# Chunked linear attention with two MLPs: loads in order of use into separate memory, and low words of the weight conversion in PSUM banks

## The chip, the core and the metric

The kernel runs on one core of one Trainium2 chip. The metric is the device time of one execution in microseconds (us), the median of several runs. The engines are TensorE (PE in the profile; PEld is its weight load), VectorE (DVE), ScalarE (ACT), GpSimd (POOL) and SyncE (SP), which only issues DMAs here. Each works through its own queue of instructions in order and waits for other engines by semaphores.

## The reference, cut to what matters

```python
# attention: B=2, H=8, S=768, D=64; blocks of 64 with a decaying state
intra = einsum(qb, kb) * Dmask          # lam ** (i - j), lower triangle
out   = intra @ vb + (qb * lam_pow) @ kv_state
kv_state = lam ** 64 * kv_state + (kb * rev_pow).T @ vb
x = out as [1536 tokens, 512]
# first MLP
h = x @ w_in                            # 512 -> 2048
x = (h * clip(h + 3, 0, 6) / 6) @ w_out # 2048 -> 512
# second MLP
h = x @ w2_in
P = a0 + a1 h + a2 h^2 + a3 h^3;  Q = 1 + |b0| |h| + |b1| h^2
y = (P / (Q + 1e-6)) @ w2_out
```

The four weight matrices are 64-bit floats in device memory, all other inputs 32-bit floats.

## The kernel before

**Attention.** The kernel uses chunks of 128 positions, 12 of them (6 for each batch entry), all 8 heads at once. For chunk c:
- `load_nat` issues the DMAs of q, k, v into tiles `qn`, `kn`, `vn` of which there are two each, so that a load waits until the chunk two before is done with its tile.
- `att_t`: TensorE transposes q and k into two banks (L339, L344), ScalarE copies them to `qT`, `kT`. GpSimd makes `qd` = q scaled (L349) and `kd` = k scaled (L352). Chunks 0 and 6 have no `qd`, chunks 5 and 11 no `kd`.
- `att_s`: the scores (L362) into two banks, which VectorE masks into `at` (L366, two halves).
- `att_o`: into bank X the product of the state with `qd` (L381) and of `at` with v (L389); into bank Y the product of `kd` with v (L386). In the text o(c).
- `att_state`: VectorE adds Y to the state (L398, L400); GpSimd makes the decayed state `sd` (L403).
- `att_x`: ScalarE copies X to `xh` (L413), VectorE subtracts to get the remainder `xl` (L414). Each large product is done in three passes, high by high, low by high, high by low.

t(c), s(c), at(c), qd(c) and so on in the text are these pieces for chunk c.

**Weights.** They come as jobs, `load_job(j)`: one or two blocks of 512 KB as raw 64-bit words, into tiles `raw0` and `raw1` of which there are two each. Jobs 0 and 1 have one block, the others one of w_in and one of w_out. A block is turned into two 32-bit parts in pieces:
- `conv_c`: ScalarE scales the high words (L153), VectorE clamps them (L154, "the clamp").
- `conv_s`: ScalarE reduces the low words in place in the raw tile (L176), VectorE shifts and joins (L177, two SBUF operands). `conv_l` is the same with the low words in bank X or Y (L163, L164); before, the main loop alone uses it.
- `conv_w`: VectorE puts the sign in (L194), which after `conv_s` comes from the raw tile.
- `conv_h`: ScalarE copies to the high part `wih` or `woh` ("hi", L207), GpSimd subtracts to get the low part `wil` or `wol` (L208).

**MLP steps.** `mm1(s)` multiplies input block s into bank `hb[s % 2]` (L216, L218, L220), `act1` applies the activation (L268 ScalarE, L271 VectorE), `act_fin` splits it into `gh` (L280) and `gl` (L281, GpSimd), `mm2` adds to the four `acc` banks (L235).

**Order.** Everything is under a manual schedule: each engine's queue is in program order. First attention chunks 0 to 4 (scores alternate between `acc[0:2]` and `acc[2:4]`, transposes use `hb`), then eight steps s = 0 to 7 that mix chunk 4 + s, mm1(s + 1), mm2(s - 1) and the conversion of job s + 3; here scores and transposes use X and Y. From s = 1 on TensorE runs mm1(s + 1), t(c), half of mm2(s - 1), s(c), the other half, o(c). Then comes the main loop of MLP steps alone. PSUM has eight banks: `acc` (4), `hb` (2), X, Y.

Of the kernel before, what the change touches and what calls it, by code (L numbers as in the profile page):

```python
# [19 lines left out]
LAG2 = 3  # L20
WARM = (6, 2, 3)
SIGN = 0x80000000
# [8 lines left out]
def fused_kernel(  # L31
# [51 lines left out]

    EIN, EOUT = 11, 9
    w_tiles(wp, range(EIN), range(EOUT))

# [38 lines left out]
    def load_job(j):  # L125
        if j >= len(jobs):
            return
        t = []
        for m, f in jobs[j]:
            r = rp.tile([128, KD, 128, 2], U32, name=f"raw{m % 2}")  # L130
            if m % 2 == 0:
                nc.sync.dma_start(
                    r.rearrange("p k f t -> p k (f t)"),
                    w32[m].rearrange("(k p) f -> p k f", p=128)[:, :, 256 * f : 256 * f + 256],
                )
            else:
# [172 lines left out]
    with ExitStack() as actx:  # L309
        ap = actx.enter_context(tc.tile_pool(name="ap", bufs=1))  # L310
        lamb = ap.tile([128, H], F32, name="lamb")
# [12 lines left out]
        def load_nat(c, which):  # L324
            b, s0 = c // CPB, (c % CPB) * CH
            for nm in which:
                x = ap.tile([128, H, D], F32, name=nm + "n", bufs=2)
                src = {"q": q, "k": k, "v": v}[nm]
                nc.sync.dma_start(x, src[b, :, s0 : s0 + CH, :].rearrange("h s d -> s h d"))
                nat.setdefault(c, {})[nm] = x  # L330

        def att_t(c, bk, between=None):
            qn, kn, vn = (nat[c][nm] for nm in "qkv")
            qT = ap.tile([128, NP, CH], F32, name="qT")
# [35 lines left out]

        Xv = X.rearrange("p (a b) -> p a b", a=NP)
        Yd = Y[:, 0 : 64 * NP].rearrange("p (a b) -> p a b", a=NP)
        decayed = {}

        def att_o(c):
            at, qd, kd, vn = live[c]
            cs = [slice(128 * p, 128 * p + 128) for p in range(NP)]

            if qd is not None:
                for p in range(NP):  # L380
                    nc.tensor.matmul(X[:, cs[p]], lhsT=state[:, p, :], rhs=qd[:, p, :], start=p == 0, stop=False,  # L381
                                     skip_group_check=True)
            halves = [(p, h2, slice(64 * h2, 64 * h2 + 64)) for p in range(NP) for h2 in range(2)]
            if kd is not None:
                for p, h2, r in halves:
                    nc.tensor.matmul(Yd[r, p, :], lhsT=kd[:, 2 * p + h2, :], rhs=vn[:, 2 * p + h2, :],  # L386
                                     start=True, stop=True)
            for p, h2, r in halves:
                nc.tensor.matmul(X[r, cs[p]], lhsT=vn[:, 2 * p + h2, :], rhs=at[:, h2, p, :],  # L389
                                 start=qd is None and p == 0, stop=p == NP - 1, skip_group_check=True)  # L390

        def att_state(c):
            if c % CPB == CPB - 1:
                return
            for h2 in range(2):
                r = slice(64 * h2, 64 * h2 + 64)
# [11 lines left out]
        def att_x(c):  # L408
            del live[c]
            o = CH * (c % CPT)  # L410
            hi = xh[c // CPT][:, :, o : o + CH]
# [4 lines left out]
        with tc.manual_schedule():  # L416
            load_nat(0, "qk")
            nc.scalar.dma_start(lamb, lam.unsqueeze(0).to_broadcast([128, H]))
            load_nat(1, "qk")
            load_nat(0, "v")  # L420
            nc.vector.memset(warm, 0.0)
            nc.vector.memset(c3, 3.0)
# [10 lines left out]

            warm_up(WARM[0])
            for h2 in range(2):
                r = slice(64 * h2, 64 * h2 + 64)
                nc.vector.tensor_copy(lamq[r, :], lamb.rearrange("p (a b) -> p a b", b=2)[r, :, h2])
            for p in range(NP):
                nc.vector.tensor_tensor_scan(
                    out=qtab[:, p, :], data0=lamq[:, p : p + 1].to_broadcast([128, CH]), data1=zero,  # L440
                    initial=1.0, op0=ALU.mult, op1=ALU.add)
                for h2 in range(2):
                    hd = 2 * p + h2
                    nc.vector.tensor_tensor_scan(
                        out=dmat[:, h2, p, :], data0=lamb[:, hd : hd + 1].to_broadcast([128, CH]), data1=ident,
                        initial=0.0, op0=ALU.mult, op1=ALU.add)
            for h2 in range(2):
                nc.vector.tensor_copy(ktab[:, :, h2], dmat[:, h2, :, CH - 1])

# [3 lines left out]


            att_t(0, hb, lambda: warm_up(WARM[1]))
            warm_up(WARM[2])
            load_nat(2, "qk")
            load_nat(1, "v")
            att_s(0, acc[0:2])
            load_job(0)  # L460
            att_t(1, hb)
            att_o(0)
            att_state(0)
            att_x(0)
            load_nat(2, "v")
            load_nat(3, "qk")
            load_job(1)
            att_s(1, acc[2:4])
            att_t(2, hb)
            conv_all(conv_c, 0)  # L470
            conv_all(conv_s, 0)
            conv_all(conv_w, 0)
            att_o(1)
            att_state(1)
            att_x(1)
            conv_all(conv_h, 0)
            load_nat(3, "v")
            load_nat(4, "qk")
            load_job(2)
            att_s(2, acc[0:2])  # L480
            att_t(3, hb)
            conv_all(conv_c, 1)
            conv_all(conv_s, 1)
            conv_all(conv_w, 1)
            att_o(2)
            att_state(2)
            att_x(2)
            conv_all(conv_h, 1)
            load_nat(4, "v")
            load_job(3)  # L490
            load_nat(5, "qk")
            nc.sync.dma_start(a_sb, a_dram.unsqueeze(0).to_broadcast([128, 4]))
            nc.sync.dma_start(b_sb, b_dram.unsqueeze(0).to_broadcast([128, 2]))
            att_s(3, acc[2:4])
            att_t(4, hb)
            load_nat(6, "qk")
            att_o(3)
            att_state(3)
            att_x(3)
            conv_all(conv_c, 2)  # L500
            conv_all(conv_s, 2)
            load_nat(5, "v")
            att_s(4, acc[0:2])
            conv_all(conv_w, 2)
            conv_h(2, 0)
            conv_h(2, 1)

            att_steps = NCH - CPT
            for s in range(att_steps):
                c = CPT + s  # L510
                j = s + 3
                load_job(j + 1)
                if s == 0:
                    mm1(0)
                    act1(0)
                    att_o(c)
                    att_state(c)
                    att_x(c)
                    act_fin(0)
                    conv_all(conv_c, j)  # L520
                    conv_all(conv_s, j)
                    mm1(1)
                    act1(1)
                else:
                    mm1(s + 1)
# [8 lines left out]
                    if s == 1:  # L534
                        conv_all(conv_w, j - 1)
                    conv_all(conv_h, j - 1)
# [4 lines left out]
                    conv_all(conv_s, j)  # L541
                    mm2(s - 1, (2, 3))
                    att_o(c)
                    att_state(c)
                    att_x(c)
# [5 lines left out]
    wq = ctx.enter_context(tc.tile_pool(name="wq", bufs=1))  # L551
    w_tiles(wq, range(EIN, NF), range(EOUT, NF))
# [92 lines left out]
```

## Time and profile before

| | |
|---|---|
| median of 3 runs | 602.67 us (602.53 to 602.83) |
| profiled execution | 602.82 us, span of its instructions 600.9 us |
| busy, share of the span | PE 588.1 us (98%), PEld 480.6 (80%), DVE 445.2 (74%), ACT 384.0 (64%), POOL 366.8 (61%) |
| granted TensorE clock | 1.00 in all slices |
| DMA | 46.68 MB, mean 78 GB/s; 39104 of 61289 packets under 512 B |

Matmuls are pipelined, so one matmul's row lasts longer than the distance to the next; the start times tell the pace. In rows of a timeline the columns are start, duration, engine, line, operation, output and inputs, count, and in brackets the idle time before with what ended it. "<-" in a row of waits separates who waited from what it waited for.

### The profile page before, as it was taken

What the parts mean: (1) busy time and instruction counts of PE and PEld (TensorE: products, weight loads), DVE (VectorE), ACT (ScalarE), POOL (GpSimd) and SP (SyncE); (2) the same over time, 40 slices, a digit from 0 to 9 for tenths busy, and PEclk for the clock granted to TensorE, in tenths of its full rate; (3) what the DMA queues carried; (4) which work ended last, traced back from release to release, by engine and by line L of the source; (5) the groups of instructions that cost most, each with busy time, mean ns of one, the idle gap of its engine ahead of it and who ended that gap; (6) DMA issues with size and microseconds to landing.
All of it is one profiled execution on the core that took longest, in us unless ns stands there. A gap on an engine that the chain in (4) does not pass through costs nothing.

```text
span 600.9 us, 8288 instructions
## 1 busy us (share of the span) xinstructions
PE 588.1 (98%) x3035; PEld 480.6 (80%) x3035; DVE 445.2 (74%) x476; ACT 384.0 (64%) x635; POOL 366.8 (61%) x291
## 2 busy tenths in 40 slices
PE   8898999999999999999999999999999999999997
PEld 5786888888888888888888787877788888888886
DVE  5877888787411011488888899999999888999991
ACT  2566465677422222588787877787887767877771
POOL 3756677566421222266676677688776677777772
PEclk9999999999999999999999999999999999999999
DMA  8987755364000000266655000000010000100001
GB/s 169 267 214 196 173 157 160 130 211 150 1 1 0 1 0 1 88 206 197 184 171 172 1 1 35 1 0 2 28 43 0 2 0 2 69 2 0 1 1 71
DMA packets 61289, 46.68 MB, mean 78 GB/s; under 512 B 39104, under 2 KB 55744, under 8 KB 61248
## 3 DMA queue, kind: packets, MB, share of 16 engines
q1 hardware_dynamic: 60960, 46.02, 26.9%
q8 instruction: 24, 0.39, 0.3%
q10 hardware_dynamic: 288, 0.14, 0.1%
q14 instruction: 17, 0.14, 0.1%
HBM read 43.00 MB, written 3.15 MB: 77 GB/s over the span
## 4 chain that ended last, share of the span: by engine, by line
PE 52%; DVE 24%; ACT 4%; issue 3%; POOL 1%; DVEq 0%; ACTq 0%
PE acc L235 26%; DVE Y L304 8%; PE hb L216 8%; PE hb L220 8%; PE hb L218 8%; DVE ta L154 2%; DVE X L164 2%; DVE ta L194 2%; DVE Y L164 2%; DVE tb L294 2%; DVE tb L194 2%; ACT ta L153 1%; DVE td L305 1%; DVE tb L154 1%; DVE raw L184 1%
## 5 line engine op out<-in xcount | busy, mean ns | idle before, releaser
L304 DVE RECIPROCAL Y<-tb 128x512 f32<-128x512 f32 x48 | 161.3, 3360 | 1.6
L281 POOL TENSOR_TENSOR gl<-td,gh 128x512 fp32r<-128x512 f32 x84 | 111.2, 1324 | 77.1 <-ACT gh L280 76.0
L216 PE MATMUL hb<-xh,wih 128*128 128x512 f32 x384 | 104.3, 393 | 0.5 <-ACT td L293 0.4
L218 PE MATMUL hb<-xh,wil 128*128 128x512 f32 x384 | 102.7, 389 | 0.0
L220 PE MATMUL hb<-xl,wih 128*128 128x512 f32 x384 | 102.6, 389 | 0.0
L295 POOL TENSOR_TENSOR tc<-ta,tc 128x512 f32<-128x512 f32 x48 | 62.2, 1295 | 58.2 <-ACT tc L292 58.2
L271 DVE SCALAR_TENSOR_TENSOR td<-tc,hb 128x512 f32<-128x512 f32 x48 | 32.8, 683 | 84.3 <-ACT tc L268 84.3
L216 PEld LDWEIGHTS hb<-xh,wih 128*128 128x128 f32 x384 | 71.1, 188 | 17.4 <-ACT td L293 1.8
L218 PEld LDWEIGHTS hb<-xh,wil 128*128 128x128 f32 x384 | 72.1, 188 | 15.2
L220 PEld LDWEIGHTS hb<-xl,wih 128*128 128x128 f32 x384 | 72.1, 188 | 15.0
L268 ACT ACTIVATE tc<-hb,c 128x512 f32<-128x512 f32 x48 | 32.9, 686 | 71.7 <-PE hb L220 71.6
L235 PE MATMUL acc<-gh,woh 128*128 128x512 f32 x192 | 76.1, 396 | 0.0
L235 PE MATMUL acc<-gl,woh 128*128 128x512 f32 x192 | 74.8, 390 | 0.0
L235 PE MATMUL acc<-gh,wol 128*128 128x512 f32 x192 | 74.8, 389 | 0.0
L280 ACT CAST gh<-td 128x512 fp32r<-128x512 f32 x84 | 52.0, 619 | 25.9 <-DVE td L271 13.8
L296 POOL TENSOR_TENSOR td<-td,tc 128x512 f32<-128x512 f32 x48 | 63.8, 1330 | 3.8
L208 POOL TENSOR_TENSOR wil<-ta,wih 128x512 fp32r<-128x512 f32 x32 | 41.4, 1294 | 34.7 <-ACT wih L207 34.7
L289 ACT ACTIVATE X<-hb,b_sb 128x512 f32<-128x512 f32 x48 | 31.8, 662 | 42.8 <-PE hb L220 34.1
L235 PE MATMUL acc<-woh,gl 128*128 128x512 f32 x144 | 56.5, 392 | 1.1 <-POOL gl L281 1.1
L235 PE MATMUL acc<-woh,gh 128*128 128x512 f32 x144 | 56.2, 390 | 0.3 <-ACT raw L253 0.3
L235 PE MATMUL acc<-wol,gh 128*128 128x512 f32 x144 | 56.0, 389 | 0.0
L208 POOL TENSOR_TENSOR wol<-tb,woh 128x512 fp32r<-128x512 f32 x29 | 38.4, 1324 | 14.4 <-ACT woh L207 14.4
(104 smaller groups left out, 1029.1 us busy)
## 6 DMA issues: line engine op xcount, KB each, us to landing
raw<-in_moe_w_in_dram SPq DMA_DIRECT2D x32, 512.0 KB, 3.8
raw<-in_moe_w_out_dram SPq DMA_DIRECT2D x32, 512.0 KB, 4.6
qn<-in_q_dram SPq DMA_DIRECT2D x12, 256.0 KB, 5.5
kn<-in_k_dram SPq DMA_DIRECT2D x12, 256.0 KB, 5.3
vn<-in_v_dram SPq DMA_DIRECT2D x12, 256.0 KB, 4.8
out_dram<-raw SPq DMA_DIRECT2D x11, 256.0 KB, 2.2
out_dram<-raw ACTq DMA_DIRECT2D x1, 128.0 KB, 1.8
out_dram<-raw SPq DMA_DIRECT2D x1, 128.0 KB, 1.7
```

The source lines that it names most:

```text
L208: nc.gpsimd.tensor_tensor(lo, x, hi.bitcast(F32), op=ALU.subtract)
L216: nc.tensor.matmul(h, lhsT=ih[:, kk, :], rhs=xh[tb][:, kk, :], start=kk == 0, stop=False)
L218: nc.tensor.matmul(h, lhsT=il[:, kk, :], rhs=xh[tb][:, kk, :], start=False, stop=False)
L220: nc.tensor.matmul(h, lhsT=ih[:, kk, :], rhs=xl[tb][:, kk, :], start=False, stop=kk == KD - 1)
L235: nc.tensor.matmul(acc[d], lhsT=l, rhs=r, start=st and i == 0, stop=sp and i == 2)
L268: nc.scalar.activation(t, h, AF.Relu, bias=c3)
L271: nc.vector.scalar_tensor_tensor(out=g, in0=t, scalar=6.0, in1=h, op0=ALU.min, op1=ALU.mult)
L280: nc.scalar.copy(gh, g)
L281: nc.gpsimd.tensor_tensor(gl, g, gh.bitcast(F32), op=ALU.subtract)
L295: nc.gpsimd.tensor_tensor(b1, h2, b1, op=ALU.mult)
L296: nc.gpsimd.tensor_tensor(a1, a1, b1, op=ALU.add)
L304: nc.vector.reciprocal(Y, q1)
```

## The change

- Loads: chunks 0 to 3 (q, k, v) and the w_in block of job 2 get tiles of their own in a new pool `pp`. All loads up to chunk 5 and job 2 are issued at the top, in the order in which they are used. To make room, only weight blocks 0 to 4 of w_in have their place from the start; blocks 5 to 10 get theirs in the memory of `pp`, which is given back in step 0. The attention's pool and the late weights lie on the other side of the memory.
- Start: 8, 3 and 2 warm-up matmuls instead of 6, 2 and 3; VectorE makes `dmat` and `ktab` ahead of `qtab`.
- `att_t` is split: `att_d` issues `qd` and `kd` at a place of its own.
- Chunks 0 to 3: o(c) alternates between X, Y and `acc[2:4]`, scores always use `acc[0:2]`. Jobs 0 and 1 are converted between the operations of chunks 2 and 3, one chunk later than before.
- Step 0: job 2 and all of job 3 are converted here, with low words in `acc[2]` and `acc[3]`.
- Steps 1 to 7: `conv_l` with low words in the two `hb` banks takes the place of `conv_s`; the pieces stand between the parts of `att_o`, `att_x` and `att_state`; `att_x` comes ahead of `att_state`. `load_job(j + 1)` is issued later in the step.

```diff
-WARM = (6, 2, 3)
+WARM = (8, 3, 2)
...
-    EIN, EOUT = 11, 9
-    w_tiles(wp, range(EIN), range(EOUT))
+    EARLY, EIN, EOUT = 5, 11, 9
+    w_tiles(wp, range(EARLY), range(EOUT))
+    pre = ExitStack()
+    pp = pre.enter_context(tc.tile_pool(name="pp", bufs=1))
...
-            r = rp.tile([128, KD, 128, 2], U32, name=f"raw{m % 2}")
+            if j == 2 and m == 0:
+                r = pp.tile([128, KD, 128, 2], U32, name="raw2")
+            else:
+                r = rp.tile([128, KD, 128, 2], U32, name=f"raw{m % 2}")
...
-    def conv_l(j, i):
+    def conv_l(j, i, bank=None):
...
-        y = (X, Y)[i].bitcast(U32).rearrange("p (a b) -> p a b", a=KD)
+        y = (bank or (X, Y)[i]).bitcast(U32).rearrange("p (a b) -> p a b", a=KD)
...
-                x = ap.tile([128, H, D], F32, name=nm + "n", bufs=2)
+                if c < CPT:
+                    x = pp.tile([128, H, D], F32, name=f"{nm}n{c}")
+                else:
+                    x = ap.tile([128, H, D], F32, name=nm + "n", bufs=2)
...
+            live[c] = qT, kT
+
+        def att_d(c):
+            (qT, kT), (kn, vn) = live[c], (nat[c][nm] for nm in "kv")
             qd = kd = None
...
-        def att_o(c):
+        def att_o(c, bk=(X, Y)):
...
             load_nat(1, "qk")
             load_nat(0, "v")
+            load_nat(2, "qk")
+            load_nat(1, "v")
+            load_nat(3, "qk")
+            load_job(0)
+            load_nat(2, "v")
+            load_job(1)
+            load_nat(4, "qk")
+            load_nat(3, "v")
+            load_job(2)
+            load_nat(4, "v")
+            load_nat(5, "qk")
...
+            S, O = acc[0:2], ((X, Y), acc[2:4])
             att_t(0, hb, lambda: warm_up(WARM[1]))
+            att_d(0)
             warm_up(WARM[2])
...
+            for c in range(CPT):
+                j = c - 2
+                att_s(c, S)
+                if j >= 0:
+                    conv_c(j, 0)
+                    conv_s(j, 0)
+                att_t(c + 1, hb)
+                att_o(c, O[c % 2])
+                if c < CPT - 1:
+                    att_d(c + 1)
+                att_state(c)
+                if j >= 0:
+                    conv_w(j, 0)
+                att_x(c)
+                if j >= 0:
+                    conv_h(j, 0)
+                if j == 0:
+                    load_job(3)
+                    load_nat(5, "v")
...
+            att_d(CPT)
             load_nat(6, "qk")
...
+            att_s(CPT, S)
...
                 if s == 0:
+
                     mm1(0)
+                    conv_all(conv_c, 2)
                     act1(0)
+                    conv_l(2, 0, acc[2])
                     att_o(c)
+                    conv_w(2, 0)
+                    act_fin(0)
+                    conv_h(2, 0)
+                    att_x(c)
                     att_state(c)
...
+                    conv_l(2, 1, acc[3])
+                    conv_w(2, 1)
                     mm1(1)
                     act1(1)
+                    conv_h(2, 1)
+                    load_job(j + 1)
+                    conv_all(conv_c, j)
+                    conv_l(j, 0, acc[2])
+                    conv_w(j, 0)
+                    conv_l(j, 1, acc[3])
+                    conv_w(j, 1)
+                    pre.close()
+                    wr = ctx.enter_context(tc.tile_pool(name="wr", bufs=1))
+                    w_tiles(wr, range(EARLY, EIN), ())
                 else:
...
+                    att_d(c)
+                    conv_all(conv_h, j - 1)
...
+                    load_job(j + 1)
                     mm2(s - 1, (0, 1))
                     act_fin(s + 1)
                     att_s(c, (X, Y))
+
                     conv_all(conv_c, j)
-                    conv_all(conv_s, j)
+                    conv_l(j, 0, hb[s % 2])
                     mm2(s - 1, (2, 3))
                     att_o(c)
+                    conv_w(j, 0)
+                    att_x(c)
                     att_state(c)
-                    att_x(c)
-                    conv_all(conv_w, j)
+                    conv_l(j, 1, hb[(s + 1) % 2])
+                    conv_w(j, 1)
```

## Rows read from the trace of the kernel before

**Rows 1.** Waits of TensorE, 0 to 140 us: total, times, longest in us.
```profile
PE X L381 <- DVE xl L414: 2.4, 2, 1.8
PE X L339 <- DVE xl L414: 1.5, 2, 1.2
```
**Rows 2.** Timeline of TensorE: scores of chunks 0 to 4, mm1(2), mm1(3).
```profile
9.26 1.69 PE L362 MATMUL acc<-qT,kT 64*128 64x128 f32 x16
...
13.40 1.26 PE L362 MATMUL acc<-qT,kT 64*128 64x128 f32 x16
...
18.00 1.26 PE L362 MATMUL acc<-qT,kT 64*128 64x128 f32 x16
...
23.93 1.26 PE L362 MATMUL acc<-qT,kT 64*128 64x128 f32 x16
...
30.55 1.26 PE L362 MATMUL acc<-qT,kT 64*128 64x128 f32 x16
...
39.92 1.07 PE L216 MATMUL hb<-xh,wih 128*128 128x512 f32 x4
...
50.50 1.19 PE L216 MATMUL hb<-xh,wih 128*128 128x512 f32 x4
```
**Rows 3.** Timeline of GpSimd and VectorE in chunk 2.
```profile
22.90 1.46 POOL L349 TENSOR_TENSOR qd<-qT,qtab 128x512 f32<-128x512 f32 x1
...
23.32 1.59 DVE L177 SCALAR_TENSOR_TENSOR ta<-ta,raw 128x512 uint32<-128x512 uint32 x1
```
**Rows 4.** Timeline of step 3, from its mm1(4) to the next step's mm1(5).
```profile
61.44 1.20 PE L216 MATMUL hb<-xh,wih 128*128 128x512 f32 x4
...
62.00 0.68 DVE L177 SCALAR_TENSOR_TENSOR tb<-tb,raw 128x512 uint32<-128x512 uint32 x1
...
69.31 1.48 POOL L208 TENSOR_TENSOR wol<-tb,woh 128x512 fp32r<-128x512 f32 x1
...
69.57 1.49 DVE L154 TENSOR_SCALAR tb<-tb 128x512 f32<-128x512 f32 x1
...
71.81 1.20 PE L216 MATMUL hb<-xh,wih 128*128 128x512 f32 x4
```
**Rows 5.** Windows of 1 us: stretch, length, granted clock, DMA share, GB/s.
```profile
7.00:8.00 1.00, 1.00 1.25 227
...
10.00:11.00 1.00, 1.00 0.01 1
```
**Rows 6.** VectorE's groups, 10 to 32 us: count, busy us, mean ns, idle before.
```profile
L366 DVE TENSOR_TENSOR at<-acc,dmat 128x512 f32<-128x512 f32 x8 | 5.1, 681 | 1.8 <-PE acc L362 1.8
...
L414 DVE TENSOR_TENSOR xl<-X,xh 128x512 fp32r<-128x512 f32 x4 | 2.8, 692 | 1.2 <-ACT xh L413 1.1
L398 DVE TENSOR_TENSOR state<-sd,Y 64x256 f32<-64x256 f32 x6 | 2.5, 416 | 0.9 <-PE Y L386 0.8
```
**Rows 7.** Timeline of GpSimd around qd of chunk 4.
```profile
28.28 1.27 POOL L208 TENSOR_TENSOR wil<-ta,wih 128x512 fp32r<-128x512 f32 x1
...
29.50 1.27 POOL L349 TENSOR_TENSOR qd<-qT,qtab 128x512 f32<-128x512 f32 x1
```
**Rows 8.** Timeline of VectorE in the main loop: conversion with the low words in X.
```profile
119.80 0.70 DVE L164 SCALAR_TENSOR_TENSOR X<-ta,X 128x512 uint32<-128x512 uint32 x1
120.53 0.69 DVE L194 SCALAR_TENSOR_TENSOR ta<-ta,X 128x512 uint32<-128x512 uint32 x1
```
**Rows 9.** Timeline: second clamps of steps 2 and 7, mm1(8) and mm1(9).
```profile
59.97 1.51 DVE L154 TENSOR_SCALAR tb<-tb 128x512 f32<-128x512 f32 x1
...
103.86 1.20 PE L216 MATMUL hb<-xh,wih 128*128 128x512 f32 x4
...
112.23 1.49 DVE L154 TENSOR_SCALAR tb<-tb 128x512 f32<-128x512 f32 x1
113.94 1.20 PE L216 MATMUL hb<-xh,wih 128*128 128x512 f32 x4
```
**Rows 10.** Timeline of ScalarE in step 1.
```profile
44.28 0.64 ACT L280 CAST gh<-td 128x512 fp32r<-128x512 f32 x1
```

More of the change, by code (lines that the diff above doesn't have):

```diff
@@ L309, in fused_kernel @@
     with ExitStack() as actx:
-        ap = actx.enter_context(tc.tile_pool(name="ap", bufs=1))
+        ap = actx.enter_context(tc.tile_pool(name="ap", bufs=1, side="right"))
         lamb = ap.tile([128, H], F32, name="lamb")
@@ L332, in att_t @@
         def att_t(c, bk, between=None):
-            qn, kn, vn = (nat[c][nm] for nm in "qkv")
+            qn, kn = (nat[c][nm] for nm in "qk")
             qT = ap.tile([128, NP, CH], F32, name="qT")
@@ L369, in att_s @@
             live[c] = (at, qd, kd, vn)
-        Xv = X.rearrange("p (a b) -> p a b", a=NP)
-        Yd = Y[:, 0 : 64 * NP].rearrange("p (a b) -> p a b", a=NP)
+        outs = {}
         decayed = {}
-        def att_o(c):
+        def att_o(c, bk=(X, Y)):
             at, qd, kd, vn = live[c]
+            ox, Yd = bk[0], bk[1][:, 0 : 64 * NP].rearrange("p (a b) -> p a b", a=NP)
+            outs[c] = ox.rearrange("p (a b) -> p a b", a=NP), Yd
             cs = [slice(128 * p, 128 * p + 128) for p in range(NP)]
@@ L380, in att_o @@
                 for p in range(NP):
-                    nc.tensor.matmul(X[:, cs[p]], lhsT=state[:, p, :], rhs=qd[:, p, :], start=p == 0, stop=False,
+                    nc.tensor.matmul(ox[:, cs[p]], lhsT=state[:, p, :], rhs=qd[:, p, :], start=p == 0, stop=False,
                                      skip_group_check=True)
@@ L388, in att_o @@
             for p, h2, r in halves:
-                nc.tensor.matmul(X[r, cs[p]], lhsT=vn[:, 2 * p + h2, :], rhs=at[:, h2, p, :],
+                nc.tensor.matmul(ox[r, cs[p]], lhsT=vn[:, 2 * p + h2, :], rhs=at[:, h2, p, :],
                                  start=qd is None and p == 0, stop=p == NP - 1, skip_group_check=True)
@@ L394, in att_state @@
                 return
+            Yd = outs[c][1]
             for h2 in range(2):
@@ L409, in att_x @@
             del live[c]
+            Xv = outs[c][0]
             o = CH * (c % CPT)
@@ L434, in fused_kernel @@
             warm_up(WARM[0])
+            for hd in range(H):
+                nc.vector.tensor_tensor_scan(
+                    out=dmat[:, hd % 2, hd // 2, :], data0=lamb[:, hd : hd + 1].to_broadcast([128, CH]), data1=ident,
+                    initial=0.0, op0=ALU.mult, op1=ALU.add)
+            for h2 in range(2):
+                nc.vector.tensor_copy(ktab[:, :, h2], dmat[:, h2, :, CH - 1])
             for h2 in range(2):
@@ L441, in fused_kernel @@
                     initial=1.0, op0=ALU.mult, op1=ALU.add)
[L442 to L448, printed above, removed]
             def conv_all(f, j, *a):
@@ L452, in conv_all @@
                     f(j, i, *a)
+            S, O = acc[0:2], ((X, Y), acc[2:4])
             att_t(0, hb, lambda: warm_up(WARM[1]))
+            att_d(0)
             warm_up(WARM[2])
[L457 to L495, printed above, removed]
-            load_nat(6, "qk")
[L497 to L506, printed above, removed]
+            for c in range(CPT):
[17 more added lines that the diff above has]
+                    load_nat(5, "v")
+                    nc.sync.dma_start(a_sb, a_dram.unsqueeze(0).to_broadcast([128, 4]))
+                    nc.sync.dma_start(b_sb, b_dram.unsqueeze(0).to_broadcast([128, 2]))
@@ L531, in fused_kernel @@
                         act1(s + 1, lambda: att_t(c, (X, Y)))
+                    att_d(c)
+                    conv_all(conv_h, j - 1)
                     if c + 2 < NCH:
                         load_nat(c + 2, "qk")
-                    if s == 1:
-                        conv_all(conv_w, j - 1)
-                    conv_all(conv_h, j - 1)
+                    load_job(j + 1)
                     mm2(s - 1, (0, 1))
@@ L540, in fused_kernel @@
                     conv_all(conv_c, j)
-                    conv_all(conv_s, j)
+                    conv_l(j, 0, hb[s % 2])
                     mm2(s - 1, (2, 3))
                     att_o(c)
+                    conv_w(j, 0)
+                    att_x(c)
                     att_state(c)
-                    att_x(c)
-                    conv_all(conv_w, j)
+                    conv_l(j, 1, hb[(s + 1) % 2])
+                    conv_w(j, 1)
                 if c + 2 < NCH:
@@ L549, in fused_kernel @@
             conv_all(conv_h, j)
-    wq = ctx.enter_context(tc.tile_pool(name="wq", bufs=1))
+    wq = ctx.enter_context(tc.tile_pool(name="wq", bufs=1, side="right"))
     w_tiles(wq, range(EIN, NF), range(EOUT, NF))
```

3 lines of the change are left out of this document (removed).

## The prediction

> **What bounds the kernel now.** I read the page first: TensorE is busy for nearly all of the span, so a change is worth only the TensorE time that it frees or blocks. Next the waits of TensorE in the first 140 us, where all the edited code runs. Hardly any is for a load: the entries that matter are for VectorE's `xl`, which releases bank X, 2.4 us ahead of the state products (L381) and 1.5 us ahead of the transposes (L339) [rows 1]. Then TensorE's timeline, to see at what pace the stages go. Chunk 1 goes from its scores (13.40) to those of chunk 2 (18.00) in 4.60 us without a wait; chunk 2 takes 5.93 us and chunk 3 6.62 us for the same instructions. That is 3.35 us lost, the most that re-ordering these two can return. The later steps are nearly full: step 1, from mm1(2) at 39.92 to mm1(3) at 50.50, takes 10.58 us [rows 2]. Last, VectorE and GpSimd side by side, since they hold each other up. An L177, which reads two SBUF tiles, took 1.59 us because GpSimd's `qd` was running until 24.36 [rows 3]; undisturbed the same instruction takes 0.68. The clamps (L154) suffer in the same way: the second of a step takes 1.49 us while `wol` runs from 69.31 to 70.79 [rows 4].
>
> **Part 1, loads.** Chunks 0 to 3 and job 2 get tiles of their own, so SP issues some 20 loads without waiting for a buffer. Before, the stream runs at 227 GB/s and then dries up (1 GB/s at 10 to 11 us): six loads are in, and the next waits for a buffer [rows 5]. At 227 GB/s 256 KB takes 1.15 us and 512 KB 2.3 us. Counted on from 10.0 us in the new order that puts k3 at 14.6, k4 at 22.7, v3 at 23.8, job 2 at 28.4 and v4 at 29.6. At the pace of 4.60 us per chunk the needs are t(3) at 19.2, t(4) at 23.8, o(3) at 25.6 and o(4) after 31. No load is late, and none was before, so the part is worth 0 in itself. What hides the loads is the attention of the chunks ahead; if the order made k4 2 us later, 1 us of it would show at t(4).
>
> **Part 2, the start.** The eighth warm-up ends before q0 is there; the third of the middle group shifts k's transposes by one matmul, and the last group gives that matmul back. [...] I take -0.4, nearer to none, since the idle stretch before q0 stays. [...]
>
> **Part 3, chunks 2 to 4.** With two pairs of output banks TensorE no longer waits for `xl` at L381. What is late next comes out of walking the queues. On VectorE, chunk 2 has the masking `at` (two of 0.68, done at 20.6), the clamp, L177, state (two of 0.42), `conv_w`, `xl` (0.69) and the next `at` [rows 6]. GpSimd wants `qd(3)` and `kd(3)`, 1.3 us each or a little less, at the same time from 20.6 on, and these take turns with the clamp, L177 and `conv_w` as in [rows 3]. If the clamp gets in ahead of `qd(3)`, at(3) ends at 26.2, else at 27.0; o(3) wants it at 26.1. Chunk 3 then goes on with the clamp behind `wil(0)` (27.0 or 27.8), L177 (27.6, 28.4), state (28.4, 29.2) and conv_w(1) (29.0, 29.8). Here one call has moved: `att_d(4)` now stands behind `sd(3)` and `wil(1)` on GpSimd. Before, `qd(4)` started at 29.50 [rows 7]. Now it follows conv_w(1), ScalarE's `hi` (0.6) and `wil(1)`, 1.27 us [rows 7], and a clamp of job 2 that waits for the same turn: it starts at 31.55 or 32.4. o(4), which TensorE could begin at 31.25 or 32.1, waits for its end, 32.9 or 33.7, and 0.3 more for `kd(4)`. With 5.6 us for o(4) and mm1(1), mm1(2) starts at 38.55 or 39.4 instead of 39.92 [rows 2]: -1.4 or -0.5. I take -1.0. The ends are -3.35, if VectorE and GpSimd never collide, and 0.
>
> **Part 4, the banks in steps 2 to 7.** `conv_l(j, 0)` puts its word into the hb bank that the next step's mm1 writes. Before, no conversion touched hb here. mm1 must now wait for `conv_w(j, 0)`, and everything of the next step stands behind mm1 on TensorE. In VectorE's queue `conv_l` comes after both clamps. The second clamp ends at 71.06 (69.57 + 1.49), as GpSimd's `wol` is in its way [rows 4], and nothing that times it is moved: `at` follows the scores, and `qd`, `kd`, `wil`, `wol` follow the transposes without a gap. Behind it come the two bitwise instructions; in the main loop, where they already use banks, they start 0.73 us apart and the second takes 0.69 [rows 8]. Less 0.08 of overlap at the front, and with 0.05 for the semaphore, mm1 can start 1.39 us after the clamp's end, at 72.45. It started at 71.81 [rows 4]: +0.64. A full step is then 10.37 + 0.64 = 11.0 us. The four full ones (chunks 7 to 10) now average (103.86 - 61.44) / 4 = 10.60 [rows 4, 9], since some lose time at L339 that the earlier `xl` returns: +0.4 each, +1.6. Step 2 (chunk 6, no `qd`, so less for TensorE): the clamp ends at 61.48, so mm1 could start at 62.87 instead of 61.44, +1.43, less the 1.2 us that its transposes waited [rows 1, 4, 9]: +0.2. Step 7 (chunk 11, no `kd`): the clamp ends at 113.72, so 115.11 instead of 113.94 [rows 9], less 0.2 for L339: +1.0. Together +2.8, between +1.3 (half of the wait) and +4.
>
> Such a bitwise instruction takes 0.70 us with an operand in a bank and 0.68 without, undisturbed [rows 4, 8]; the 0.70 is in the sum. [...]
>
> **Part 5, step 1.** `gl(1)` now goes ahead of `qd(5)` on GpSimd. Its `gh` was done at 44.92, 5.0 us after mm1(2) started [rows 2, 10]. Then `gl`, `qd` and `wil` of 1.3 us each, to 8.9; the first clamp; `wol`, 1.5; the second clamp ends at 10.7 and mm1(3) starts at 12.1 after mm1(2). It was 10.58 [rows 2]: +1.5. If the first clamp slips in ahead of `wil`, the second ends at 9.3, and it is +0.1. I take +1.4; ends 0 and +1.9.
>
> **At nothing.** The early weights in other memory: they are written long after its last reader. Raw tiles released sooner, now by ScalarE's conversion: SP issues the next load up to 2 us sooner, and ScalarE's conversions did not wait for loads in these steps; were one late, it would cost just that lateness. `att_d` apart from `att_t` in the steps: GpSimd's order stays. `xl` ahead of state: the next state products come in the following step.
>
> **Sum.** -0.4 - 1.0 + 1.4 + 2.8 = +2.8. The profiled execution took 602.82 us for a span of 600.9, 0.15 over the median of the three runs, 602.67. So 602.67 + 2.8, 605.4 us.
>
> **Rivals.** *The conversions are freed (faster).* Its place is VectorE's second clamp. Two of the three conversion instructions now have an operand in PSUM, and in the main loop that form takes 0.70 us where L177 took up to 1.59 [rows 3, 8]. If GpSimd, not held up, runs so far ahead that `wol` is over when the clamp comes, the clamp ends 1.1 us sooner, conv_w is done before mm1 wants its bank, and the waits at L381 and L339 go. It decides from 0.64 us of advance in a full step. Then it is -0.4, -2.0 for the chunks, -0.5 for step 1 and -0.2 to -0.4 in each later step: -4.5, 598.2. Against it: L177 comes after the clamps, and GpSimd's chain starts with the transposes, so neither moves the collision. [...] Chance 0.20.
>
> *It cancels.* The chunks return 2 us more than I take, -3 in all, and the banks cost what I say: 602.67 - 0.4 - 3 + 1.4 + 2.8 = 603.5, or 602.2 if step 1 costs only 0.1. For it: 3.35 us are there. Against it: `qd(4)` behind `wil(1)`. It also covers a change that does not do what it says because its loads were hidden anyway. Chance 0.18.
>
> *The forecast*, mm1 held by its bank: 0.62, with 603.9 to 607.2 as its own range.
>
> **Range and chances.** 0.2%, 1.2 us, is about what a measurement of this kernel can tell from no change. The forecast lies above that, the first rival below, the second within: faster 0.20, same 0.18, slower 0.62. The range, 600.6 to 607.4, takes in most of the upper ends of parts 4 and 5, the case that cancels and the near edge of the first rival.
>
> **What would show it.** A wait of L216 for VectorE's L194, 0.5 to 1.4 us in each of seven steps, and steps of 11.0 us; second clamps still at 1.5 us; no wait for `xl` at L381; L381 of chunk 4 waiting for GpSimd's `qd`; mm1(2) near 38.5. If mm1 starts without that wait, or the second clamp takes 0.4 us, the forecast is wrong.

## The result, and the profile after

| | kernel before | changed kernel |
|---|---|---|
| median | 602.65 us (602.53 to 602.83, 4 runs) | 608.38 us (606.75 to 609.04, 4 runs) |
| ratio | | 1.0091 [1.0071, 1.0111] |
| profiled execution | 602.82 us, span 600.9 | 608.38 us, span 606.7 |

The change makes the kernel slower by 5.7 us. The forecast had the sign and the wait of mm1 for its bank, but only +2.8, and the time lies 1.0 us above its range. The line numbers have moved: the first mm1 line L216 is now L221, its other two L223 and L225; mm2 is L240, the clamp L159, `conv_l` L169, the sign L199, `wil` and `wol` L213, `gl` L286, transposes L347 and L352, `qd` L361, scores L374, state products L394, v L399 and L402, `xh` L428, `xl` L429.

The waits of TensorE in the changed kernel, 0 to 140 us:

```profile
PE hb L221 <- DVE ta L199: 5.5, 5, 2.2
PE hb L221 <- ACT hb L168: 1.3, 1, 1.3
...
PE hb L221 <- ACT xh L428: 0.7, 1, 0.7
PE acc L399 <- DMA vn<-in_v_dram: 0.5, 1, 0.5
PE X L394 <- POOL qd L361: 0.3, 1, 0.3
```

The two entries of [rows 1] for `xl` are gone. In their place mm1 waits for its bank, seven times, 7.5 us in all. Five of these are named as waits for L199. The other two belong to the same instruction, as the times will show. Next, TensorE's timeline:

```profile
7.54 1.26 PE L374 MATMUL acc<-qT,kT 64*128 64x128 f32 x16 [0.24 <-ACT kT L353]
...
16.62 1.26 PE L374 MATMUL acc<-qT,kT 64*128 64x128 f32 x16
...
31.23 1.16 PE L394 MATMUL X<-qd,state 128*128 128x128 f32 x8 [0.31 <-POOL qd L361]
...
36.75 1.07 PE L221 MATMUL hb<-xh,wih 128*128 128x512 f32 x4
...
49.22 2.01 PE L221 MATMUL hb<-xh,wih 128*128 128x512 f32 x4 [2.17 <-DVE ta L199]
51.03 1.85 PE L223 MATMUL hb<-xh,wil 128*128 128x512 f32 x4
...
53.64 0.60 PE L347 MATMUL X<-ident,qn 128*128 128x128 f32 x4
...
61.84 1.15 PE L221 MATMUL hb<-xh,wih 128*128 128x512 f32 x4 [1.49 <-DVE ta L199]
...
72.93 1.16 PE L221 MATMUL hb<-xh,wih 128*128 128x512 f32 x4 [0.68 <-ACT xh L428]
...
106.06 1.17 PE L221 MATMUL hb<-xh,wih 128*128 128x512 f32 x4 [0.61 <-DVE ta L199]
...
117.34 1.15 PE L221 MATMUL hb<-xh,wih 128*128 128x512 f32 x4 [1.31 <-ACT hb L168]
```

Set against [rows 2, 4, 9], the lead or lag of the changed kernel is -1.72 us at the scores of chunk 0, -1.38 at those of chunk 2, -3.17 at mm1(2), -1.28 at mm1(3), +0.40 at mm1(4), +1.12 at mm1(5), +2.20 at mm1(8), +3.40 at mm1(9) and +5.8 at the end. So the first 37 us win 3.2 us, the seven steps lose 6.6, and the main loop, whose code the diff does not touch, loses another 2.4. That makes three places to explain.

### The profile page after: what moved, and what is told of

Same layout as the page of the kernel before. It is cut to its first block, busy times and chain, and to the rows that moved or that the text cites. A ratio compares the mean times of both kernels' runs of the same rounds, so it can differ in the third digit from the quotient of the medians.

```text
span 606.7 us, 8289 instructions
## 1 busy us (share of the span) xinstructions
PE 591.3 (97%) x3037; PEld 481.4 (79%) x3037; DVE 440.9 (73%) x476; ACT 383.2 (63%) x635; POOL 367.6 (61%) x291
## 4 chain that ended last, share of the span: by engine, by line
PE 65%; DVE 20%; ACT 5%; issue 5%; SPq 3%; POOL 1%; DMA 1%; DVEq 0%; ACTq 0%; POOLq 0%
PE acc L240 31%; PE hb L221 11%; PE hb L223 10%; PE hb L225 10%; DVE Y L309 4%; DVE ta L159 3%; DVE ta L199 2%; SPq L337 2%; DVE X L169 2%; ACT ta L158 2%; DVE tb L199 2%; DVE Y L169 2%; DMA vn<-in_v_dram 1%; DVE tb L159 1%; DVE tb L299 1%
## 5 line engine op out<-in xcount | busy, mean ns | idle before, releaser
L286 POOL TENSOR_TENSOR gl<-td,gh 128x512 fp32r<-128x512 f32 x84 | 111.1, 1323 | 80.5 <-ACT gh L285 79.2
L221 PE MATMUL hb<-xh,wih 128*128 128x512 f32 x384 | 105.3, 396 | 7.7 <-DVE ta L199 5.5
L223 PE MATMUL hb<-xh,wil 128*128 128x512 f32 x384 | 103.9, 393 | 0.0
L225 PE MATMUL hb<-xl,wih 128*128 128x512 f32 x384 | 103.0, 390 | 0.0
L221 PEld LDWEIGHTS hb<-xh,wih 128*128 128x128 f32 x384 | 71.6, 189 | 25.4 <-ACT hb L168 5.6
L223 PEld LDWEIGHTS hb<-xh,wil 128*128 128x128 f32 x384 | 72.7, 189 | 15.7
L225 PEld LDWEIGHTS hb<-xl,wih 128*128 128x128 f32 x384 | 72.2, 188 | 15.5
L240 PE MATMUL acc<-gh,woh 128*128 128x512 f32 x192 | 76.4, 398 | 0.0
L240 PE MATMUL acc<-gh,wol 128*128 128x512 f32 x192 | 75.2, 392 | 0.0
L240 PE MATMUL acc<-gl,woh 128*128 128x512 f32 x192 | 74.8, 390 | 0.0
L213 POOL TENSOR_TENSOR wil<-ta,wih 128x512 fp32r<-128x512 f32 x32 | 41.8, 1306 | 30.2 <-ACT wih L212 30.1
L240 PE MATMUL acc<-woh,gl 128*128 128x512 f32 x144 | 56.8, 394 | 0.8 <-POOL gl L286 0.8
L240 PE MATMUL acc<-woh,gh 128*128 128x512 f32 x144 | 56.5, 392 | 0.0
L240 PE MATMUL acc<-wol,gh 128*128 128x512 f32 x144 | 56.4, 391 | 0.0
L213 POOL TENSOR_TENSOR wol<-tb,woh 128x512 fp32r<-128x512 f32 x29 | 38.6, 1330 | 19.5 <-ACT woh L212 19.5
```

The lines of the kernel that those rows point to most:

```text
L213: nc.gpsimd.tensor_tensor(lo, x, hi.bitcast(F32), op=ALU.subtract)
L221: nc.tensor.matmul(h, lhsT=ih[:, kk, :], rhs=xh[tb][:, kk, :], start=kk == 0, stop=False)
L223: nc.tensor.matmul(h, lhsT=il[:, kk, :], rhs=xh[tb][:, kk, :], start=False, stop=False)
L225: nc.tensor.matmul(h, lhsT=ih[:, kk, :], rhs=xl[tb][:, kk, :], start=False, stop=kk == KD - 1)
L240: nc.tensor.matmul(acc[d], lhsT=l, rhs=r, start=st and i == 0, stop=sp and i == 2)
L286: nc.gpsimd.tensor_tensor(gl, g, gh.bitcast(F32), op=ALU.subtract)
```

## Where the time went, in the trace

**The steps.** All engines in step 3, to be read beside [rows 4]:

```profile
69.14 0.63 ACT L168 ACTIVATE hb<-raw 128x512 uint32<-128x512 uint32 x1
69.73 1.44 POOL L213 TENSOR_TENSOR wol<-tb,woh 128x512 fp32r<-128x512 f32 x1
69.97 1.48 DVE L159 TENSOR_SCALAR tb<-tb 128x512 f32<-128x512 f32 x1
...
71.38 0.68 DVE L169 SCALAR_TENSOR_TENSOR hb<-ta,hb 128x512 uint32<-128x512 uint32 x1
72.10 0.69 DVE L199 SCALAR_TENSOR_TENSOR ta<-ta,hb 128x512 uint32<-128x512 uint32 x1
...
72.30 0.59 ACT L428 CAST xh<-X 128x512 fp32r<-128x512 f32 x1 [2.53 <-PE X L402]
```

The second clamp still takes 1.48 us behind `wol`. ScalarE's part of the conversion (L168) is done at 69.77, so what holds up L169 is the clamp ahead of it in VectorE's queue. L169 and L199 follow it, and mm1(5) starts at 72.93, 0.14 after L199's end at 72.79. In step 1 the distance is the same 0.14: L199 ends at 49.08 and mm1(3) starts at 49.22. The `xh` named for mm1(5) only happens to end in between (72.89), and for mm1(9), named for L168, L199 ends at 117.20, again 0.14 ahead of 117.34. From the clamp's end to mm1 it is 1.48 us here and 1.47 in step 1, where the forecast had 1.39. The step's length, 72.93 - 61.84 = 11.09, was forecast as 11.0.

**The clock.** Step 1 ends in a wait of 2.17 us. TensorE's own windows there show what follows (stretch, length, busy, granted clock, DMA share, GB/s):

```profile
46.00:48.00 2.00, 1.05 (x17) 1.00 0.71 278
48.00:50.00 2.00, 0.78 (x2) 0.82 0.59 137
50.00:52.00 2.00, 2.00 (x6) 0.50 0.00 0
52.00:54.00 2.00, 2.00 (x11) 0.83 0.00 0
```

The granted clock goes from 1.00 to 0.50. mm1(3) takes 2.01 us for its four matmuls where mm1(2) took 1.07, and its twelve matmuls take 53.64 - 49.22 = 4.42 us. Three of the four runs have a mean clock of 0.996 or 0.997 (608.38 to 609.04 us); the fourth has 1.000 and took 606.75. Only the profiled run shows where its clock fell. A lower mean is not new either: 6 of the 18 runs of the kernel before beside experiments 1 to 4 have 0.997, and took 602.78 to 604.27 us.

**The main loop.** First mm1 passes of four successive steps in the changed kernel:

```profile
204.78 1.07 PE L221 MATMUL hb<-xh,wih 128*128 128x512 f32 x4
...
210.22 1.07 PE L221 MATMUL hb<-xh,wih 128*128 128x512 f32 x4
...
215.66 1.08 PE L221 MATMUL hb<-xh,wih 128*128 128x512 f32 x4
...
221.16 1.08 PE L221 MATMUL hb<-xh,wih 128*128 128x512 f32 x4
```

No step waits for anything, and the steps take 5.44, 5.44 and 5.50 us. The last of these is the first step on late weights (blocks 11 to 15 of w_in), and the four behind it are as slow. Where these lie is one of the things the diff changes: they begin at byte 180192 of each partition, where they began at 179488, so 704 bytes higher.

## The experiments

Each kernel ran beside the kernel before on the same chip; that one's medians there were 602.75 (experiments 1 to 4), 602.87 (5 to 8) and 602.91 us (9 to 12), on three chips. In the expectations a letter or name of a theory belongs to the run whose expectation uses it.

**1. The late weights back at their old address**, in the changed kernel.

```diff
-    wq = ctx.enter_context(tc.tile_pool(name="wq", bufs=1, side="right"))
+    wq = ctx.enter_context(tc.tile_pool(name="wq", bufs=1))
```

> The changed kernel with the late weight blocks (w_in 11 to 15, w_out 9 to 15) at byte 179488 of each partition, where the kernel before has them, instead of 704 bytes higher. Theory A (the place of these tiles sets TensorE's pace): the main loop's steps that use them return from 5.49 to 5.60 us to 5.44, and the time falls by 2.0 to 2.6 us against the changed kernel, to about 606. Theory B (the slower steps are a condition of the chip or of a throttle in that run, or come from other engines): the same steps stay slow, or are slow in other places, and the time stays at 608.4 within 0.6 us.

605.86 us (605.1 to 606.12), 1.005 [1.0035, 1.0065]: 2.5 us less than the changed kernel. The steps from above, and mm1(3) with the transposes that end it:

```profile
49.74 1.16 PE L221 MATMUL hb<-xh,wih 128*128 128x512 f32 x4 [2.17 <-DVE ta L199]
...
52.59 0.60 PE L347 MATMUL X<-ident,qn 128*128 128x128 f32 x4
...
214.33 1.07 PE L221 MATMUL hb<-xh,wih 128*128 128x512 f32 x4
...
219.77 1.07 PE L221 MATMUL hb<-xh,wih 128*128 128x512 f32 x4
```

The step on late weights is back at 5.44 us, and from mm1(9), at 116.31, to the end of the span, 603.3, it is 486.99 us, as before (600.9 - 113.94 = 486.96); the changed kernel took 489.36. The profiled run also shows the same wait of 2.17 us without a fall of the clock: mm1(3) takes 52.59 - 49.74 = 2.85 us, 1.57 less than above. The other three runs have a clock of 0.996 or 0.997 and took 605.78 to 606.12 us; where it fell in them is not traced.

**2. The kernel before with the late weights moved alone.**

```diff
-    wq = ctx.enter_context(tc.tile_pool(name="wq", bufs=1))
+    wq = ctx.enter_context(tc.tile_pool(name="wq", bufs=1, side="right"))
```

> The kernel before with only its late weight blocks moved up by 704 bytes, as in the changed kernel. Theory A (place of the tiles): 2.0 to 2.6 us slower than before, about 605, with main loop steps of 5.49 to 5.60 us where blocks 11 to 15 are used, and nothing else changed. Theory B: same time as before within 0.3 us.

605.40 us (605.01 to 606.22), 1.0046 [1.0031, 1.0061]. One step on late weights:

```profile
213.32 1.08 PE L216 MATMUL hb<-xh,wih 128*128 128x512 f32 x4
...
218.81 1.08 PE L216 MATMUL hb<-xh,wih 128*128 128x512 f32 x4
```

5.49 us again, and up to 5.60 in the second MLP. From mm1(9) at 114.92 to the end of the span at 604.3 it is 489.38 us, as in the changed kernel. One keyword, which moves no instruction in any queue, costs 2.4 us there. The medians differ by 2.65, but three of these four runs have a mean clock of 0.996 or 0.997, and in the profiled one it falls to 0.50 after a wait of 1.80 us:

```profile
27.36 1.13 PE L381 MATMUL X<-qd,state 128*128 128x128 f32 x8 [1.80 <-DVE xl L414]
```

**3. The bank's conversion ahead of the second clamp**, in the changed kernel. The second block's scaling on ScalarE, which is part of `conv_c`, moves with its clamp.

```diff
-                    conv_all(conv_c, j)
+                    conv_c(j, 0)
                     conv_l(j, 0, hb[s % 2])
...
                     att_x(c)
                     att_state(c)
+                    conv_c(j, 1)
                     conv_l(j, 1, hb[(s + 1) % 2])
```

> The changed kernel with one move in steps 1 to 7: the clamp of the job's second block goes behind the first block's conversion and the attention's output, instead of ahead of it. Theory A (mm1 waits for its bank because the second clamp stands in front of the conversion and is held up by GpSimd): the waits of mm1 for conv_w fall from 0.6 to 2.2 us to under 0.3 in each step, the full step from 11.05 to about 10.45 us, TensorE's clock does not fall after step 1, and the time drops by 5 to 7 us, to about 602. Theory B (the bank itself costs the time, wherever the clamp stands): waits of 0.5 us and more stay, and the time drops by under 2 us.

601.09 us (600.47 to 601.73, 9 runs), 0.9971 [0.9961, 0.9981]: 7.3 us less than the changed kernel, and faster than the kernel before although the late weights are still misplaced. Its waits of TensorE, 0 to 140 us, hold one entry for L199, for 0.94 us in step 1 and 0.28 in step 2:

```profile
PE hb L221 <- DVE ta L199: 1.2, 2, 0.9
```

Its step 3, and the start of the mm1 behind step 4:

```profile
57.51 1.16 PE L221 MATMUL hb<-xh,wih 128*128 128x512 f32 x4 [0.28 <-DVE ta L199]
...
65.44 1.46 POOL L213 TENSOR_TENSOR wol<-tb,woh 128x512 fp32r<-128x512 f32 x1
...
65.86 0.70 DVE L169 SCALAR_TENSOR_TENSOR hb<-ta,hb 128x512 uint32<-128x512 uint32 x1
66.59 0.69 DVE L199 SCALAR_TENSOR_TENSOR ta<-ta,hb 128x512 uint32<-128x512 uint32 x1
...
67.88 1.20 PE L221 MATMUL hb<-xh,wih 128*128 128x512 f32 x4
...
70.09 0.43 DVE L159 TENSOR_SCALAR tb<-tb 128x512 f32<-128x512 f32 x1
...
78.28 0.96 PE L221 MATMUL hb<-xh,wih 128*128 128x512 f32 x3
```

L169 runs at 0.70 us right beside `wol`, L199 is done at 67.28, 0.60 before mm1 starts, and the second clamp, now after `wol`, takes 0.43 us. Step 3 takes 67.88 - 57.51 = 10.37 and step 4 78.28 - 67.88 = 10.40, which is TensorE's own work (the forecast had 10.37). So `wol` does not slow L169, which has one of its two inputs in a bank (0.70 us here beside `wol`, 0.70 for that form in [rows 8]), while the clamp takes 1.48 us beside `wol` in the changed kernel and 0.43 behind it here. Why the two differ, no run here shows.

**4. The warm-ups alone**, in the kernel before.

```diff
-WARM = (6, 2, 3)
+WARM = (8, 3, 2)
```

> The kernel before with the warm-up matmuls 8, 3, 2 instead of 6, 2, 3, nothing else. Theory A (the eight warm-ups bring TensorE's upper clock level before the first transposes): chunk 0's scores start about 1.2 to 1.7 us earlier than at 9.26 and take 1.26 us; how much of it reaches the end depends on the loads, which stay in the old order: 0.3 to 1.4 us faster. Theory B (the earlier start of the changed kernel came from its loads): scores start at 9.2 or later, same time.

603.15 us (10 runs), 1.0004 [0.9995, 1.0013]: no difference. Its timeline of TensorE:

```profile
7.35 1.26 PE L362 MATMUL acc<-qT,kT 64*128 64x128 f32 x16 [0.24 <-ACT kT L345]
...
18.95 0.66 PE L339 MATMUL hb<-ident,qn 128*128 128x128 f32 x4 [1.11 <-DMA qn<-in_q_dram]
...
27.49 1.13 PE L381 MATMUL X<-qd,state 128*128 128x128 f32 x8 [1.78 <-DVE xl L414]
```

The kernel before, at the same L381:

```profile
28.00 1.13 PE L381 MATMUL X<-qd,state 128*128 128x128 f32 x8 [1.78 <-DVE xl L414]
```

The scores of chunk 0 are 1.91 us sooner than in [rows 2], but now the transposes wait for a load, and L381 waits for `xl` as in [rows 1]. There 0.51 us of the lead is left (27.49 against 28.00). After the 1.78 us the granted clock of this run falls to 0.50 between 30 and 32 us, and mm1(2) starts at 41.01, 13.52 us behind L381. In the kernel before, where the same wait of 1.78 us is followed by no fall, it is 11.92. The four runs with a mean clock of 0.999 or 1.000 took 602.52 to 603.16 us, so without a fall the start gains nothing either.

**5. Both repairs**, experiments 1 and 3 together.

> The changed kernel with both edits: the second clamp behind the first block's conversion, and the late weights at the address that the kernel before gives them. Theory A (the two losses are separate): their gains add up, 601.1 - 2.4 = 598.7, main loop steps of 5.44 us. Theory B (one hides the other): 600 or more.

598.80 us (598.37 to 599.4), 0.9929 [0.9914, 0.9943]: the two gains add up (601.09 - 2.4 = 598.7). The next experiments start from this kernel or from that of experiment 1.

**6. No banks in the steps**: experiment 1 with the low words of steps 1 to 7 in the raw tile.

```diff
-                    conv_l(j, 0, hb[s % 2])
+                    conv_s(j, 0)
...
-                    conv_l(j, 1, hb[(s + 1) % 2])
+                    conv_s(j, 1)
```

> The changed kernel with late weights at the old address, but in steps 1 to 7 the low words are reduced in the raw tile in SBUF as before, at the same places in the order, both clamps first. Theory A (only the tie between mm1 and a bank costs): no wait of mm1 for a conversion, full steps of 10.4 to 10.6 us, 600 to 601 in all, as contention with GpSimd returns. Theory B (the interleaved order itself delays the steps): steps stay at 11.0, total at 605.

601.18 us (600.74 to 602.52), 0.9972 [0.9959, 0.9984]. mm1 no longer waits, and the wait for `xl` at the transposes is back:

```profile
PE X L347 <- DVE xl L429: 1.9, 3, 1.6
```

Against this kernel the banks cost 605.86 - 601.18 = 4.7 us with both clamps ahead of the conversion (3.9 to the profiled run of experiment 1, where the clock does not fall), and the kernel with banks in the order of experiment 3 is 601.18 - 598.80 = 2.4 us faster than this one. So banks can be had without the loss; the place in VectorE's queue decides. Whether the 2.4 us come from the banks or from the order alone is not shown, as the raw tile in the order of experiment 3 was not run.

**7. Shared tiles for all chunks**: experiment 5 with q, k, v of chunks 0 to 3 in the two shared tiles of each name.

```diff
-                if c < CPT:
+                if c < 0:
```

> As the kernel with both repairs, but q, k, v of chunks 0 to 3 go through the two shared tiles each again, in the new order of issue. Theory A (with the start 1.7 us sooner the loads do bind, and separate memory is what carries the gain): TensorE waits for loads in chunks 2 and 3, step 1 starts 1.5 to 4 us later, the total is up by the same. Theory B (loads are hidden by attention anyway, as forecast): under 0.5 us.

598.56 us, 0.9931 [0.9912, 0.995], against 598.80. SP's queue now waits for buffers at the load's line (0 to 40 us), and TensorE doesn't notice:

```profile
SPq L337 <- POOL kd L364: 3.3, 2, 1.9
SPq L337 <- PE hb L352: 2.0, 3, 1.0
```

Its mm1(2) starts at 36.80, the same as with tiles of their own. The separate tiles of q, k and v are worth nothing; job 2 kept its own tile here, so that one is not tested.

**8. to 10. Where the late weights lie**: experiment 5 with 64 bytes ahead of the late weights, with 256 bytes there, and with 64 bytes ahead of all weights and of x, so that all tiles of the main loop move together.

```diff
+    pad = ctx.enter_context(tc.tile_pool(name="pad", bufs=1))
+    pad.tile([128, 16], F32, name="pad")       # 64 bytes; [128, 64] for 256
     wq = ctx.enter_context(tc.tile_pool(name="wq", bufs=1))
```

> As the kernel with both repairs, with the late weights 64 bytes higher (179552). Theory A (what counts is how these tiles lie to a multiple of 128 bytes): steps of blocks 11 to 15 at 5.49 and 5.56 us again, as with 704 bytes. Theory B (only a larger offset, or the 2048-byte pattern, counts): 5.44.

> As the kernel with both repairs, with the late weights 256 bytes higher (179744). Theory A (the pattern repeats within 256 bytes): steps of blocks 11 to 15 at 5.44 us. Theory B (it takes the full 2048 bytes that the other tiles share): 5.47 to 5.60 us.

> As the kernel with both repairs, with weights, activations and all other main loop tiles moved up by the same 64 bytes, so that the late weights lie at 179552 as in the run that was slow, but their distance to the other tiles is as before. Theory A (what counts is the distance between the tiles that TensorE reads together): all main loop steps at 5.44 us, 598.8. Theory B (what counts is each tile's own alignment): all steps of the main loop slow, 5.5 to 5.6, the time up by 8 us or more.

Single runs: 602.70 us with 64 bytes, 598.85 with 256, 598.83 with all tiles moved by 64. With 64 bytes a step on late weights reads

```profile
208.39 1.09 PE L221 MATMUL hb<-xh,wih 128*128 128x512 f32 x4
...
213.99 1.09 PE L221 MATMUL hb<-xh,wih 128*128 128x512 f32 x4
```

5.60 us. With all tiles moved (its lines are two further down) it is 5.44:

```profile
207.82 1.07 PE L223 MATMUL hb<-xh,wih 128*128 128x512 f32 x4
...
213.26 1.07 PE L223 MATMUL hb<-xh,wih 128*128 128x512 f32 x4
```

With 256 it is 5.44 too (207.50 to 212.94). With all tiles moved the late weights lie at the very address that was slow with 64 bytes. So it is not their own address that counts but their distance from the other tiles of the main loop, and 256 bytes more are as good as none. Which of the other tiles it is, and why, these runs do not show.

**11. k scaled earlier**: experiment 5 with `att_d` of chunk 4 in the loop, like those of the other chunks.

```diff
-                if c < CPT - 1:
-                    att_d(c + 1)
+                att_d(c + 1)
...
-            att_d(CPT)
```

> As the kernel with both repairs, with att_d of chunk 4 at the place in the loop where the others stand, ahead of the decayed state and of the low part of job 1. Theory A (qd and kd of chunk 4 are held up behind these): the wait of L394 for qd, 0.3 to 0.5 us, goes, and that of L399 too; 0.3 to 0.9 us faster than with both repairs. Theory B (the low part of job 1 then comes late for mm1(1), or nothing changes): 598.8 or more.

598.35 us (598.23 to 598.43), 0.9926 [0.9911, 0.9941], the lowest median of all. The wait for chunk 4's `qd` is gone and mm1(2) starts at 35.90 instead of 36.80, but in step 1 the scores then wait 0.48 us for `kT`. ScalarE, which copies it, had to wait for the load of the second MLP's b, and works without a break from there to `kT`:

```profile
36.79 0.20 ACT L574 ACTIVATE b1a<-b_sb 128x1 f32<-128x1 f32 x1 [1.59 <-DMA b_sb<-in_moe_b_dram]
```

So mm1(3) starts at 47.80, only 0.24 us sooner than in experiment 5 (48.04). The 0.45 us to experiment 5 are not resolved: its runs begin at 598.37.

**12. The old warm-ups**: experiment 5 with `WARM = (6, 2, 3)`.

> As the kernel with both repairs, with the warm-up matmuls 6, 2, 3 of the kernel before. Theory A (the warm-ups bring the start forward, and with the loads in the new order it is kept): scores of chunk 0 back at about 9.2 us, 1.2 to 1.7 us slower, 600.0 to 600.5. Theory B (the loads or VectorE catch up): 598.8 to 599.3.

599.16 us (598.6 to 600.53), 0.9936 [0.992, 0.9953]. The scores of chunk 0 start at 8.79 instead of 7.21, those of chunk 2 at 17.19 instead of 16.29, mm1(2) at 37.37 instead of 36.80. In the profiled run, the slowest of the four, the same load comes later still, and mm1(3) starts at 49.81:

```profile
38.97 0.20 ACT L576 ACTIVATE b1a<-b_sb 128x1 f32<-128x1 f32 x1 [3.22 <-DMA b_sb<-in_moe_b_dram]
```

By the medians 0.4 us are left at the end, which these runs do not resolve.

## Why the prediction was wrong, point by point

| term, us | forecast | measured in the profiled run |
|---|---|---|
| start (to the scores of chunk 2) | -0.4 | -1.4 |
| chunks 2 to 4 (to mm1(2)) | -1.0 | -1.8 |
| step 1 | +1.4 | +1.9 |
| banks in steps 2 to 7 | +2.8 | +3.1 |
| clock after the wait of step 1 | not in the sum | +1.6 |
| main loop (late weights) | nothing | +2.4 |
| sum | +2.8 | +5.8 |

**The step that failed first** is "At nothing". It priced the early weights' new memory by the time at which they are written, and it did not price the late weights' move at all. A tile's place was taken to matter only through buffers that are still in use. Experiments 1 and 2 show the place itself: 2.4 us in the traces, both when it is taken back and when it is moved alone, with every instruction the same. Experiments 8 to 10, single runs, show that the distance to the other tiles decides. What in the memory makes it so was not found.

**The second** is that no term stood for the clock. Part 5 forecast a late mm1(3) and priced the wait alone. After the 2.17 us of it the granted clock fell to 0.50 in the profiled run, which costs 1.57 us by the same twelve matmuls in experiment 1; two more of the four runs have the same low mean. It is not the wait's length alone, since experiment 1 shows 2.17 us without a fall. In the profiled runs of experiments 3 and 5 to 12 the longest wait of TensorE in these steps is 1.6 us (experiment 6), the others stay under 1 us, and no run of these kernels has a mean clock under 0.999. Why the clock falls in some executions of one program and not in others, no run here shows.

With only one of the two the time lies in the range: experiment 1 took 605.86, and the run of the changed kernel whose mean clock is 1.000 took 606.75. The four terms that the forecast did price came to +1.8 together, for +2.8: the start and the chunks 1.8 us better than it had, the steps 0.8 worse. So it is luck that experiment 1 lies near the forecast's 605.4.

**Part 1** (loads worth nothing): right for the memory of q, k and v, by experiment 7. One load is late after all, chunk 3's v, by the 0.5 us of L399. The part did not look at the load of b. ScalarE waits for it for 0.84 us in the changed kernel (L575, at 36.22), ahead of step 1's start, and then for mm1(1), so it costs nothing there; but in experiments 11 and 12 it comes after that start and holds up step 1.

**Part 2** (start): the -0.4 was my estimate, and no run shows it. In the two profiled runs chunk 0's scores take 1.26 us instead of the 1.69 of [rows 2], and all ahead of them is quicker: they start 1.72 us sooner, and 1.38 of it is left at the scores of chunk 2. The granted clock reads 1.00 from 2 to 10 us in both runs, so it does not show what makes them quicker. How much sooner they start varies from execution to execution: the scores start at 8.65 to 9.26 us in the three profiled runs with six warm-ups, and at 7.21 to 8.27 in those with eight. And experiments 4 and 12 show how little of a start's lead reaches the end: none in the kernel before, 0.4 us unresolved in experiment 5.

**Part 3** (chunks): o(4) waits for `qd` of chunk 4, as forecast, which comes right behind `wil` (28.45 and 29.70 for 31.55). The walk along the queues gave 38.55 for mm1(2) in its better branch. Less the start's 1.4 to 1.7 us that is 36.8 to 37.2, and 36.75 was measured. I had taken a value between the branches and too little for the start.

**Part 4** (banks): the mechanism is right in each part: a second clamp of 1.48 us, conversions of 0.68 and 0.69, mm1 held by L199, steps of 11.03 to 11.09 for 11.0. The distance from the clamp to mm1 was 0.08 to 0.09 us longer than forecast in each step: from L199's end to mm1 it is 0.14, where the forecast had 0.05 for the semaphore. Over six steps that is more than the +0.3. Experiment 3 shows the cause: with only the second block's scaling and clamp moved, the wait goes but for steps 1 and 2. Experiment 6 gives the size of the banks' part, 3.9 us by the traces (from mm1(2) to mm1(9) 79.24 us in experiment 1, 75.31 in experiment 6), where parts 4 and 5 forecast 4.2. The kernel before takes 74.02, so 1.3 us come with the new order, without any bank.

**Part 5** (step 1): 12.47 us for 12.1. The clamp ends 11.0 us after mm1(2) instead of 10.7, and the same 0.08 comes on top.

**The rivals.** "The conversions are freed" decided at the second clamp, and that clamp kept its 1.48 us. What the rival described is real, but it takes another order of VectorE's queue, which experiment 3 has: 601.09, and 598.80 with the late weights in place, near its 598.2. That is near by chance: step 1 takes 11.24 us in experiment 5, 0.66 more than before, where the rival had it 0.5 shorter. "It cancels" asked for 3.4 us from the start and the chunks; 3.2 were there, but the steps, the clock and the main loop took 9.0 (1.9 + 3.1 + 1.6 + 2.4).

**The marks it named.** The wait for L199 (2.17 us in step 1, over the 1.4 of the mark), the 1.5 us clamps, no wait for `xl`, the wait for `qd` all came; mm1(2) came at 36.75, not 38.5. None of these marks looks at the main loop, so the largest miss could not show in any of them.

## What to carry to other kernels

When an intermediate is moved into a bank that the next stage writes, everything ahead of its reader in that engine's queue becomes part of the next stage's wait: put the conversion first and let the rest follow (7.3 us here, the clock's share included). A tile that is only given another place is a change too (2.4 us here, in experiments 1 and 2): compare a stage's pace with the addresses before and after, even where no instruction differs. A long wait of TensorE may be charged twice, once as the wait and once as slow matmuls behind it (2.17 us and another 1.57 in the changed kernel; the same wait in experiment 1 was charged once).

## What the runs showed of the hardware that was not expected

- The pace of this stream of matmuls depends on the distance between the late tiles and the rest: in the first MLP 24 matmuls take 5.44 us at the old place, 5.50 at 704 bytes more, 5.60 at 64 more, and 5.44 at 256 more or when all tiles move by 64. The last three are single runs.
- The granted clock fell to 0.50 after single waits of 1.78 us (experiment 4), 1.80 us (experiment 2) and 2.17 us (the changed kernel). It did not after the same 1.78 us in the kernel before, nor after the same 2.17 us in experiment 1. A fall cost 1.57 us in the changed kernel and 1.60 in experiment 4.
- With eight warm-ups chunk 0's scores take 1.26 us in every profiled run. With six they took 1.69 us in the kernel before, 1.36 in experiment 12 and 1.26 in experiment 2, at a granted clock that reads 1.00 from 2 to 10 us in the kernel before and in experiment 12. The transposes of q ahead of them took 0.63 us in the changed kernel and 1.09 in experiment 3, both with eight warm-ups.
